# Softmax weights normalised in the output rows instead of in the probability tiles

## The chip, the cores and the metric

One core of a Trainium2 chip runs the whole program. The metric is the device time of one execution in microseconds. Times of single instructions come from one profiled execution.

## The reference

Clustered attention is followed by two MLPs. The attention has 2 batches, 8 heads, 768 positions and 64 columns a head; queries only see keys of their own cluster (the nearest of 16 centroids):

```
mask   = q_assign[:, :, :, None] == k_assign[:, :, None, :]
scores = where(mask, scale * q @ k.T, -1e9);  scores -= max(scores)
attn   = exp(scores)
attn   = attn / (sum(attn) + 1e-9)
out    = attn @ v                      # then [1536, 512]
x      = (sigmoid(x @ w_gate) * (x @ w_val)) @ w_out
x      = relu(x @ w_in)**2 @ w_out2
```

All of it is fp32 in accuracy: operands are split into a high and a low part, and products are sums of several matmuls.

## The kernel before

Heads are worked in pairs: `pairs` has 8 entries, 4 in each batch. A pair has 12 units `(i, e, n, j)`: head e of the pair, half n of the 768 query rows, and block j of 128 rows in the half. There are 96 units, and one loop over n with one iteration a unit orders the whole attention by hand (`manual_schedule`: each engine runs its instructions in the order in which the code issues them).

In iteration n the code issues, for unit n, the negated row maximum on VectorE (L934, tile nm); for the unit three iterations back (LAG = 3) two groups of three transposes on TensorE and their rounding copy on ScalarE (`evac`, L820 and L822); the scores of unit n + 1 on TensorE (L802); the exponential of unit n on ScalarE, which also sums the rows (L955); the normalisation of unit n - 1 (`normalise`: a reciprocal on VectorE, L873, and a multiplication of the 128x768 probability tile on GpSimd, L874); the low parts of the transposed tiles on VectorE (`low`, L828); and 1e-9 added to the row sums on GpSimd (L969). The transposes share a ring of three PSUM buffers (`ps_t`) with the preparation steps; the scores have two.

When the third block of a half has been transposed, three thirds of the output matmuls follow in the next three iterations (`attend`, L838 and L839). The value tile holds the high and the low part of V side by side, so an output tile has two parts of 64 rows. ScalarE copies it out of PSUM (L844), and SP moves the parts to their places (L848, L850). `finish`, some iterations later, adds the two parts on GpSimd (L858) and splits the sum into x_hi (L867) and x_lo (L869), the input of the first MLP. `SUMS` holds how many iterations later each of its steps comes.

The dictionary `late` holds work for the end of an iteration; a function that returns a `post` has that part issued at the start of the next (`drain`). The preparation of the next pair (`STEPS`; transposes of q and k, similarity to the centroids, argmax, masks) is spread over the iterations in the same way. Weight tiles of the MLPs are fetched by SP and decoded mostly on VectorE (L218 to L252); two are decoded during the first pairs of the attention, two more as it ends (`LATE_DECODES`), and the first four gated matmul groups are issued there too (`LATE_GATED`, L348 to L350). SP issues all transfers in the order of the code; a transfer that waits holds up those behind it.

Of the kernel before, what the change touches and what calls it, by code (L numbers as in the profile page):

```python
# [8 lines left out]
F32 = mybir.dt.float32  # L9
# [5 lines left out]
ALU = mybir.AluOpType  # L15
AX = mybir.AxisListType
# [44 lines left out]

EARLY_PARTS = [1, 1, 2, 2, 3, 3, 4, 9, 15, 18, 21, 22, 23, 27, 30, 31, 33, 39]
VALUES = [-3, 2, 0, 6]
SUMS = [[5, 6, 8], [6, 8, 9]]

LATE_DECODES = [1, 2]
LATE_GATED = [1, 2, 3, 3]
# [3 lines left out]
def cluster_attention_two_mlps(  # L71
# [13 lines left out]
    nc = tc.nc  # L85
    B, H, S, D = q.shape
    NCL = centroids.shape[1]
    P = 128
# [5 lines left out]
    HB = NB // 2  # L94
    NH = HB * P
# [222 lines left out]
    with tc.manual_schedule():  # L318
        ident = const.tile([P, P], F32, name="ident")
# [3 lines left out]
        ones = const.tile([P, 1], F32, name="ones")  # L323
# [129 lines left out]
        with ExitStack() as ac:  # L453
# [2 lines left out]
            nat = pc.enter_context(tc.tile_pool(name="nat", bufs=1, side="right"))  # L456
            am = pc.enter_context(tc.tile_pool(name="am", bufs=1, side="right"))
            vp = ac.enter_context(tc.tile_pool(name="vp", bufs=3))
            LAG = 3
            pp = ac.enter_context(tc.tile_pool(name="pp", bufs=LAG + 1))  # L460
            ptp = ac.enter_context(tc.tile_pool(name="ptp", bufs=2))
            sm = ac.enter_context(tc.tile_pool(name="sm", bufs=6))
            ps_t = ac.enter_context(tc.tile_pool(name="ps_t", bufs=3, space=PSUM))
            ps_o = ac.enter_context(tc.tile_pool(name="ps_o", bufs=1, space=PSUM))
            sc = ac.enter_context(ExitStack())
# [320 lines left out]


            units = [(i, e, n, j) for i in range(len(pairs)) for e in range(2) for n in range(2) for j in range(HB)]
            Pt, PThi, PTlo, xs, nms, decoding = {}, {}, {}, {}, {}, {}
            UPP, N = len(units) // len(pairs), len(units)  # L790


# [37 lines left out]
            def attend(i, e, n, third):  # L830

                if third == 0:
                    outs[i, e, n] = ps_o.tile([P, NH], F32, name="o")
                o = outs[i, e, n]
                hi, lo = PThi[i, e, n], PTlo[i, e, n]
                for c in range(third * NB // 3, (third + 1) * NB // 3):
                    vt = V[i, e][:, c].rearrange("p t d -> p (t d)")
                    nc.tensor.matmul(o, vt, hi[:, c, :], start=(c == 0), stop=False)  # L838
                    nc.tensor.matmul(o, vt, lo[:, c, :], start=False, stop=(c == NB - 1))  # L839
                if third == 2:  # L840

                    def post():
                        oc = sm.tile([P, NH], F32, name=f"oc{e}", bufs=3 - e)
                        nc.scalar.copy(oc, outs.pop((i, e, n)))  # L844
                        own, other = slice(D * e, D * e + D), slice(D - D * e, 2 * D - D * e)
                        if e == 0:
                            xs[n] = [oc, sm.tile([P, NH], F32, name="x", bufs=2)]
                        nc.sync.dma_start(out=xs[n][1][own], in_=oc[other])  # L848
                        if e == 1:
                            nc.sync.dma_start(out=xs[n][0][own], in_=oc[own])  # L850

                    return post

            def finish(i, n, t):
                b, hp = pairs[i]
                xa, xb = xs[n]
                if t == 0:
                    nc.gpsimd.tensor_tensor(out=xa, in0=xa, in1=xb, op=ALU.add)  # L858
                    return
                c0 = b * S + n * NH  # L860
                while c0 < b * S + (n + 1) * NH:
                    g = c0 // TG
                    c1 = min(b * S + (n + 1) * NH, (g + 1) * TG)
                    src = xa[:, c0 - b * S - n * NH : c1 - b * S - n * NH]
                    hi, lo = (x[:, hp, c0 - g * TG : c1 - g * TG] for x in x_in[g])
                    if t == 1:
                        nc.gpsimd.tensor_scalar(out=hi, in0=src, scalar1=1.0, scalar2=1.0, op0=ALU.mult, op1=ALU.mult)  # L867
                    else:
                        nc.gpsimd.tensor_tensor(out=lo, in0=src, in1=f32(hi), op=ALU.subtract)  # L869
                    c0 = c1  # L870

            def normalise(p, nm):
                nc.vector.reciprocal(out=nm[:, 3:4], in_=nm[:, 2:3])  # L873
                nc.gpsimd.tensor_scalar(out=p, in0=p, scalar1=nm[:, 3:4], scalar2=ones, op0=ALU.mult, op1=ALU.mult)  # L874

            load(0, "kq")
            load(1, "kq")
# [25 lines left out]
            for t, f in enumerate(prep0):  # L903
# [9 lines left out]

                keep_warm(WARM.get(t - len(prep0), 0))
            outs, late, st = {}, {}, {}
            todo = {}
            for i in range(len(pairs)):
                for m, args in zip(VALUES, ((0, 0), (0, 1), (1, 0), (1, 1))):
                    late.setdefault(max(0, i * UPP + m), []).append((values, (i, *args)))
            for i in range(1, len(pairs)):  # L920
                for m, group in (prep1 if i == 1 else prep(i)).items():
                    at = (i - 1) * UPP + m
                    todo.setdefault(at, []).append(group)
            st[0] = scores(units[0])
            for n in range(N + LAG + 4):
                u = units[n] if n < N else None
                w = units[n - LAG] if 0 <= n - LAG < N else None
                if n == N - UPP:
                    drain()
                    pc.close()  # L930
                    open_weights()
                if u is not None:
                    nms[n] = sm.tile([P, 4], F32, name="nm")
                    nc.vector.tensor_reduce(out=nms[n][:, 0:1], in_=st[n][:, :, :NH], axis=AX.XY, op=ALU.max, negate=True)  # L934
                nm = nms.pop(n - 1, None)
                if nm is not None:
                    p = Pt[units[n - 1]]
                drain()
                if nm is not None and w is None:
                    normalise(p, nm)  # L940
                if n == N:
                    sc.close()
                    for nm_, bufs in (("sg", 2), ("act", NA)):
                        pools[nm_] = ctx.enter_context(tc.tile_pool(name=nm_, bufs=bufs, side="right", reuse_waits="tile"))
                    pools["a"] = ctx.enter_context(
                        tc.tile_pool(name="ps_a", bufs=4, space=PSUM, side="right", reuse_waits="tile")
                    )
                if w is not None:
                    t0, h0 = evac(w, 0)
                    t1, h1 = evac(w, 1)  # L950
                if n + 1 < N:
                    st[n + 1] = scores(units[n + 1])
                if u is not None:
                    e = pp.tile([P, S], F32, name="p")
                    nc.scalar.activation(  # L955
                        out=e.rearrange("p (m n) -> p m n", m=2),
                        in_=st.pop(n)[:, :, :NH],
                        func=AF.Exp,
                        bias=nms[n][:, 0:1],
                        accum_out=nms[n][:, 1:2],  # L960
                    )
                    Pt[u] = e
                if w is not None:
                    if nm is not None:
                        normalise(p, nm)
                    low(w, 0, t0, h0)
                    low(w, 1, t1, h1)
                if u is not None:
                    nc.gpsimd.tensor_scalar(out=nms[n][:, 2:3], in0=nms[n][:, 1:2], scalar1=1e-9, scalar2=None, op0=ALU.add)  # L969
                if w is not None:  # L970
                    Pt.pop(w)
                    if w[3] == HB - 1:
                        end = n == N + LAG - 1
                        for t in range(3):
                            late.setdefault(n + 1 + (0 if end else t), []).append((attend, (*w[:3], t)))
                        if w[1] == 1:
                            for t in range(3):
                                at = n + SUMS[w[2]][t] if w[0] < len(pairs) - 1 else n + (3 if end else 6)
                                late.setdefault(at, []).append((finish, (w[0], w[2], t)))
                for f, args in late.pop(n, []):  # L980
                    do(f, *args)
                for m, group in enumerate(todo.pop(n, [])):
                    if m:
                        drain()
                    for f in group:
                        do(f)
                for part in decoding.pop(n, []):
                    part()
                if n - N in LATE_DECODES:
                    for t, part in enumerate(decode_next()):  # L990
                        if t < 6:
                            part()
                        else:
                            decoding.setdefault(n + 1, []).append(part)
                for t, at in enumerate(LATE_GATED):
                    if n == N + at:
                        (gated_first, gated_second)[t % 2](steps[t // 2])
# [46 lines left out]
```

## Time and profile before

| | |
|---|---|
| Median of 3 runs | 828.5 us (828.44 to 828.93) |
| Profiled execution | 829.15 us, span 827.4 us |
| TensorE matmul busy | 809.6 us (98%) |
| TensorE weight load busy | 690.7 us (83%) |
| VectorE busy | 628.4 us (76%) |
| ScalarE busy | 441.1 us (53%) |
| GpSimd busy | 214.3 us (26%), all of it in the first 280 us |

The profile comes from one execution. Matmul times overlap one another, so the rate of matmuls is read from the distance of their starts. "Idle before, releaser" gives the idle time of an engine before an instruction and whose end stopped it. PE is TensorE, PEld its weight loads, DVE VectorE, ACT ScalarE, POOL GpSimd, SPq the transfer queue of SP.

### The profile page before, as it was taken

How to read it: one execution, taken by the hardware profiler on the slowest of the kernel's cores; microseconds unless marked ns; L12 is line 12 of the kernel's file. 1: busy time of each engine (PE TensorE's matmuls, PEld its weight loads, DVE VectorE, ACT ScalarE, POOL GpSimd, SP SyncE). 2: the span in 40 equal slices, each digit the busy share in tenths (PEclk: the TensorE clock that was granted, in tenths of full speed). 3: DMA queues.
4: the chain of work that ended last, by engine and by line, in shares of the span. 5: the costliest groups of instructions: out<-in, count | busy, mean ns of one | idle time of the engine just before them, and what ended most of it. 6: DMA issues, size and time to landing. Idle time of an engine off the chain costs nothing.

```text
span 827.4 us, 11694 instructions
## 1 busy us (share of the span) xinstructions
PE 809.6 (98%) x4097; PEld 690.7 (83%) x4097; DVE 628.4 (76%) x1146; ACT 441.1 (53%) x887; POOL 214.3 (26%) x349
## 2 busy tenths in 40 slices
PE   7899999999999999999999999999999999999998
PEld 6789899999998788888888888888888888888886
DVE  6999999999898378657878757769774787788233
ACT  5778889889896223432332223246755733642530
POOL 4678899888884200000000000000000000000000
PEclk9999999999999999999999999999999999999999
DMA  8475464464321123112321212202222212221012
GB/s 198 91 158 117 98 153 104 108 139 94 81 76 37 54 70 99 51 62 69 99 77 52 77 51 77 67 10 80 74 77 76 77 51 76 77 77 52 0 51 101
DMA packets 63274, 67.01 MB, mean 81 GB/s; under 512 B 28624, under 2 KB 54224, under 8 KB 63216
## 3 DMA queue, kind: packets, MB, share of 16 engines
q1 hardware_dynamic: 63216, 66.27, 29.4%
q8 instruction: 32, 0.52, 0.3%
q14 instruction: 26, 0.21, 0.1%
HBM read 45.12 MB, written 3.15 MB: 58 GB/s over the span
## 4 chain that ended last, share of the span: by engine, by line
PE 80%; DVE 13%; POOL 2%; ACT 2%; issue 2%; DMA 1%; SPq 0%; POOLq 0%; DVEq 0%; ACTq 0%
PE bank_b L426 18%; PE bank_a L349 13%; PE bank_a L348 13%; PE bank_a L350 13%; PE bank_a L426 9%; DVE pt_lo L828 4%; PE t L820 4%; DVE nm L934 4%; PE s L802 4%; PE o L838 2%; PE o L839 2%; DMA oc<-oc 1%; PE t L617 1%; POOL p L874 1%; PE t L562 1%
## 5 line engine op out<-in xcount | busy, mean ns | idle before, releaser
L349 PE MATMUL bank_a<-x_lo,w 128*128 128x512 f32 x480 | 189.5, 395 | 0.9 <-POOL x_lo L869 0.9
L348 PE MATMUL bank_a<-x_hi,w 128*128 128x512 f32 x480 | 188.3, 392 | 0.1
L350 PE MATMUL bank_a<-x_hi,w 128*128 128x512 f32 x480 | 187.7, 391 | 0.0
L392 DVE TENSOR_TENSOR slo<-act,shi 128x512 fp32r<-128x512 f32 x84 | 57.8, 688 | 69.2 <-ACT shi L391 64.9
L348 PEld LDWEIGHTS bank_a<-x_hi,w 128*128 128x128 f32 x480 | 90.1, 188 | 21.3 <-POOL x_hi L867 0.5
L349 PEld LDWEIGHTS bank_a<-x_lo,w 128*128 128x128 f32 x480 | 90.1, 188 | 20.9 <-POOL x_lo L869 1.2
L350 PEld LDWEIGHTS bank_a<-x_hi,w 128*128 128x128 f32 x480 | 90.2, 188 | 20.1
L828 DVE TENSOR_TENSOR pt_lo<-t,pt_hi 128x384 fp32r<-128x384 f32 x192 | 96.7, 544 | 7.8 <-ACT pt_hi L822 7.7
L874 POOL TENSOR_SCALAR p<-p,nm,ones 128x768 f32<-128x768 f32 x96 | 94.9, 989 | 16.8 <-DVE nm L873 15.0
L955 ACT ACTIVATE p<-s,nm 128x768 f32<-128x768 f32 x96 | 88.0, 916 | 18.0 <-DVE nm L873 10.4
L802 PE MATMUL s<-st_k,st_q 128*128 128x384 f32 (+1 forms) x384 | 91.8, 362 | 1.9 <-ACT p L955 1.9
L934 DVE TENSOR_REDUCE nm<-s 128x1 f32<-128x768 f32 x96 | 90.8, 946 | 0.0
L822 ACT CAST pt_hi<-t 128x384 fp32r<-128x384 f32 x192 | 83.3, 488 | 6.9 <-PE t L820 6.5
L820 PE MATMUL t<-ident,p 128*128 128x128 f32 x576 | 82.2, 277 | 3.7 <-DVE pt_lo L828 2.3
L391 ACT CAST shi<-act 128x512 fp32r<-128x512 f32 x84 | 51.6, 615 | 58.2 <-PE bank_b L426 34.6
L426 PE MATMUL bank_b<-wo,shi 128*128 128x512 f32 x256 | 79.0, 390 | 0.0
L230 ACT CAST w<-wtop 128x512 fp32r<-128x512 f32 x38 | 23.7, 622 | 102.6 <-DVE wtop L248 102.6
L820 PEld LDWEIGHTS t<-ident,p 128*128 128x128 f32 x576 | 66.7, 141 | 11.2 <-issue 3.7
L374 DVE TENSOR_TENSOR act<-bank_a,sg 128x512 f32<-128x512 f32 x36 | 24.9, 691 | 55.5 <-PE bank_a L350 51.2
L802 PEld LDWEIGHTS s<-st_k,st_q 128*128 128x128 f32 (+1 forms) x384 | 63.2, 191 | 4.5 <-ACT p L955 4.2
L838 PE MATMUL o<-pt_hi,vt 128*128 128x384 f32 x192 | 65.2, 339 | 0.4 <-ACT oc L844 0.4
L839 PE MATMUL o<-pt_lo,vt 128*128 128x384 f32 x192 | 64.7, 337 | 0.0
(137 smaller groups left out, 1385.6 us busy)
## 6 DMA issues: line engine op xcount, KB each, us to landing
wraw<-in_moe_w_out_dram SPq DMA_DIRECT2D x28, 512.0 KB, 3.3
wraw<-in_moe_w_in_dram SPq DMA_DIRECT2D x16, 512.0 KB, 3.9
wraw<-in_moe_w_gate_dram SPq DMA_DIRECT2D x11, 512.0 KB, 3.6
wraw<-in_moe_w_val_dram SPq DMA_DIRECT2D x11, 512.0 KB, 3.6
nat_v<-in_v_dram SPq DMA_DIRECT2D x8, 384.0 KB, 3.4
st_k<-st_k SPq DMA_DIRECT2D x16, 192.0 KB, 4.8
x<-oc SPq DMA_DIRECT2D x32, 96.0 KB, 2.1
out_dram<-part SPq DMA_DIRECT2D x12, 256.0 KB, 2.1
```

The lines of the kernel that those rows point to most:

```text
L348: nc.tensor.matmul(bk, w[:, 0, ks], mov_hi[:, kk], start=(kk == 0), stop=False)
L349: nc.tensor.matmul(bk, w[:, 0, ks], mov_lo[:, kk], start=False, stop=False)
L350: nc.tensor.matmul(bk, w[:, 1, ks], mov_hi[:, kk], start=False, stop=(kk == KD - 1))
L426: nc.tensor.matmul(bk, st, mv, start=(first and n == 0), stop=(last and n == 2))
L802: nc.tensor.matmul(st[:, m, :NH], Q[i, e][: DEPTH[e][a], a, c * P : (c + 1) * P], K[i, e][: DEPTH[e][a], a, m * NH : (m + 1) * NH], start= ...
L820: nc.tensor.transpose(tp[:, m, :], Pt[u][:, c * P : (c + 1) * P], ident)
L822: nc.scalar.copy(hi, tp)
L828: nc.vector.tensor_tensor(out=lo, in0=tp, in1=f32(hi), op=ALU.subtract)
L838: nc.tensor.matmul(o, vt, hi[:, c, :], start=(c == 0), stop=False)
L874: nc.gpsimd.tensor_scalar(out=p, in0=p, scalar1=nm[:, 3:4], scalar2=ones, op0=ALU.mult, op1=ALU.mult)
L934: nc.vector.tensor_reduce(out=nms[n][:, 0:1], in_=st[n][:, :, :NH], axis=AX.XY, op=ALU.max, negate=True)
L955: nc.scalar.activation(out=e.rearrange("p (m n) -> p m n", m=2), in_=st.pop(n)[:, :, :NH], func=AF.Exp, bias=nms[n][:, 0:1], accum_out=nms ...
```

## The change

The probability tiles stay unnormalised. The row sums of a half, three blocks of two heads, are collected in one tile of 128x6 (`sums`). `reciprocals` does the rest in three steps, spread over iterations by `RECIPROCALS`: step 0 adds 1e-9 and takes the reciprocal on VectorE; step 1 transposes the 128x6 tile on TensorE into a buffer of `ps_t`, and its post copies it on ScalarE and writes it to DRAM as two rows of 384; step 2 reads each row back, broadcast to 64 partitions. `finish` gets a fourth step, a multiplication of the output by this tile on GpSimd. The normalisation and its reciprocals go, LAG becomes 2, and `SUMS` is set anew.

```diff
-SUMS = [[5, 6, 8], [6, 8, 9]]
+SUMS = [[6, 7, 8, 9], [6, 7, 9, 10]]
+RECIPROCALS = [(1, 4, 5), (1, 2, 3)]
...
-            LAG = 3
+            LAG = 2
...
+            rows = ac.enter_context(tc.tile_pool(name="rows", bufs=2, space=bass.MemoryType.DRAM))
...
+                if t == 1:
+                    nc.gpsimd.tensor_tensor(out=xa, in0=xa, in1=recips.pop((i, n)), op=ALU.mult)
+                    return
...
-            def normalise(p, nm):
-                nc.vector.reciprocal(out=nm[:, 3:4], in_=nm[:, 2:3])
-                nc.gpsimd.tensor_scalar(out=p, in0=p, scalar1=nm[:, 3:4], scalar2=ones, op0=ALU.mult, op1=ALU.mult)
+            def reciprocals(i, n, t):
+                if t == 0:
+                    ss = sums[i, n]
+                    nc.vector.tensor_scalar(out=ss, in0=ss, scalar1=1e-9, scalar2=None, op0=ALU.add)
+                    nc.vector.reciprocal(out=ss, in_=ss)
+                elif t == 1:
+                    tr = ps_t.tile([2 * HB, P], F32, name="t")
+                    nc.tensor.transpose(tr, sums.pop((i, n)), ident)
+                    def post():
+                        recips[i, n] = sm.tile([P, NH], F32, name="rc", bufs=2)
+                        rr = recips[i, n][: 2 * HB, :P]
+                        nc.scalar.copy(rr, tr)
+                        by_row[i, n] = rows.tile([2, NH], F32, name="r")
+                        nc.sync.dma_start(out=by_row[i, n].rearrange("e (j p) -> (e j) p", p=P), in_=rr)
+                    return post
+                else:
+                    rc = recips[i, n]
+                    src = by_row.pop((i, n))
+                    for h in range(2):
+                        nc.sync.dma_start(out=rc[D * h : D * h + D], in_=src[h : h + 1].to_broadcast([D, NH]))
...
-                        accum_out=nms[n][:, 1:2],
+                        accum_out=sums[u[0], u[2]][:, HB * u[1] + u[3] :][:, :1],
...
-                    nc.gpsimd.tensor_scalar(out=nms[n][:, 2:3], in0=nms[n][:, 1:2], scalar1=1e-9, scalar2=None, op0=ALU.add)
+                if u is not None and u[1] == 1 and u[3] == HB - 1:
+                    for t, at in enumerate((0, 1, 2) if n == N - 1 else RECIPROCALS[u[2]]):
+                        late.setdefault(n + at, []).append((reciprocals, (u[0], u[2], t)))
```

## Rows read from the trace of the kernel before

**Rows 1.** The page's first part: busy us, share of the span, instructions.
```profile
PE 809.6 (98%) x4097; PEld 690.7 (83%) x4097; DVE 628.4 (76%) x1146; ACT 441.1 (53%) x887; POOL 214.3 (26%) x349
```

**Rows 2.** Busy time by stretch: stretch, length; PE, PEld, DVE, ACT, POOL; clock, DMA, GB/s.
```profile
19.30:45.00 25.70, 21.27 (x123) 17.60 (x122) 24.80 (x48) 18.52 (x44) 16.01 (x24) 0.93 0.49 121
150.90:180.20 29.30, 29.00 (x201) 27.91 (x200) 27.33 (x59) 25.88 (x62) 25.05 (x40) 1.00 0.53 121
```

**Rows 3.** Timeline of VectorE (start, length): maxima of units 12, 24, 48 and 60.
```profile
52.55 0.95 DVE L934 TENSOR_REDUCE nm<-s 128x1 f32<-128x768 f32 x1
84.42 0.94 DVE L934 TENSOR_REDUCE nm<-s 128x1 f32<-128x768 f32 x1
143.54 0.95 DVE L934 TENSOR_REDUCE nm<-s 128x1 f32<-128x768 f32 x1
172.91 0.95 DVE L934 TENSOR_REDUCE nm<-s 128x1 f32<-128x768 f32 x1
```

**Rows 4.** Chain that ended last, in pair 4: start, us on the chain, what.
```profile
151.76 0.87 DVE nm L934
155.96 0.67 PE t L820 x6
156.63 0.71 PE s L802 x4
```

**Rows 5.** Instruction groups, first 330 us: busy us, mean ns | idle before, releasers.
```profile
L874 POOL TENSOR_SCALAR p<-p,nm,ones 128x768 f32<-128x768 f32 x96 | 94.9, 989 | 16.8 <-DVE nm L873 15.0 <-PE o L839 0.7 <-PE s L802 0.6
L873 DVE RECIPROCAL nm<-nm 128x1 f32<-128x1 f32 x96 | 14.7, 153 | 6.2 <-POOL nm L969 5.9
```

**Rows 6.** Decode lines L248 and L241, 15 to 300 us: ns min/median/max, first, last.
```profile
L248 DVE SCALAR_TENSOR_TENSOR wtop<-wmag,wbody x5: 682/693/696, 259.5 to 298.0; 128x512 f32<-128x512 f32 x5
L248 DVE SCALAR_TENSOR_TENSOR spare<-spare x2: 852/1104/1357, 26.1 to 83.6; 128x512 f32<-128x512 f32 x2
...
L241 DVE TENSOR_SCALAR wbody<-wraw x5: 416/421/1102, 258.3 to 296.8; 128x512 int32<-128x512 int32 x5
```

**Rows 7.** Timeline around the maxima of units 18 and 19.
```profile
66.76 1.01 POOL L858 TENSOR_TENSOR oc<-oc,x 128x384 f32<-128x384 f32 x1 [0.98 <-DMA oc<-oc]
...
67.28 0.94 DVE L934 TENSOR_REDUCE nm<-s 128x1 f32<-128x768 f32 x1
...
69.53 0.16 DVE L873 RECIPROCAL nm<-nm 128x1 f32<-128x1 f32 x1 [0.84 <-POOL nm L969]
...
69.61 1.00 DVE L828 TENSOR_TENSOR pt_lo<-t,pt_hi 128x384 fp32r<-128x384 f32 x2
...
71.26 0.94 DVE L934 TENSOR_REDUCE nm<-s 128x1 f32<-128x768 f32 x1
```

**Rows 8.** Timeline at the end of pair 7: maxima of units 92 to 94.
```profile
245.81 0.95 DVE L934 TENSOR_REDUCE nm<-s 128x1 f32<-128x768 f32 x1
...
248.16 0.95 DVE L934 TENSOR_REDUCE nm<-s 128x1 f32<-128x768 f32 x1
...
249.65 0.16 DVE L873 RECIPROCAL nm<-nm 128x1 f32<-128x1 f32 x1 [0.55 <-POOL nm L969]
...
250.67 0.95 DVE L934 TENSOR_REDUCE nm<-s 128x1 f32<-128x768 f32 x1
```

**Rows 9.** Timeline from the attention's end into the first MLP.
```profile
262.94 0.49 ACT L844 COPY oc<-o 128x384 f32<-128x384 f32 x1
...
267.42 0.37 SPq L192 DMA_DIRECT2D wraw<-in_moe_w_val_dram  x1
...
267.85 0.51 SPq L848 DMA_DIRECT2D x<-oc  x1
...
272.93 1.01 POOL L858 TENSOR_TENSOR oc<-oc,x 128x384 f32<-128x384 f32 x1 [15.38 <-DMA oc<-oc]
...
275.92 0.50 PE L349 MATMUL bank_a<-x_lo,w 128*128 128x512 f32 x1 [0.88 <-POOL x_lo L869]
```

**Rows 10.** The page's part on transfers: count, KB each, median us to landing.
```profile
x<-oc SPq DMA_DIRECT2D x32, 96.0 KB, 2.1
```

More of the change, by code (lines that the diff above doesn't have):

```diff
@@ L788, in cluster_attention_two_mlps @@
             units = [(i, e, n, j) for i in range(len(pairs)) for e in range(2) for n in range(2) for j in range(HB)]
-            Pt, PThi, PTlo, xs, nms, decoding = {}, {}, {}, {}, {}, {}
+            Pt, PThi, PTlo, xs, decoding = {}, {}, {}, {}, {}
             UPP, N = len(units) // len(pairs), len(units)
@@ L846, in post @@
                         if e == 0:
-                            xs[n] = [oc, sm.tile([P, NH], F32, name="x", bufs=2)]
-                        nc.sync.dma_start(out=xs[n][1][own], in_=oc[other])
+                            xs[i, n] = [oc, sm.tile([P, NH], F32, name="x", bufs=2)]
+                        nc.sync.dma_start(out=xs[i, n][1][own], in_=oc[other])
                         if e == 1:
-                            nc.sync.dma_start(out=xs[n][0][own], in_=oc[own])
+                            nc.sync.dma_start(out=xs[i, n][0][own], in_=oc[own])
                     return post
@@ L855, in finish @@
                 b, hp = pairs[i]
-                xa, xb = xs[n]
+                xa, xb = xs[i, n]
                 if t == 0:
                     nc.gpsimd.tensor_tensor(out=xa, in0=xa, in1=xb, op=ALU.add)
+                    return
+                if t == 1:
+                    nc.gpsimd.tensor_tensor(out=xa, in0=xa, in1=recips.pop((i, n)), op=ALU.mult)
                     return
@@ L865, in finish @@
                     hi, lo = (x[:, hp, c0 - g * TG : c1 - g * TG] for x in x_in[g])
-                    if t == 1:
+                    if t == 2:
                         nc.gpsimd.tensor_scalar(out=hi, in0=src, scalar1=1.0, scalar2=1.0, op0=ALU.mult, op1=ALU.mult)
@@ L915, in cluster_attention_two_mlps @@
             outs, late, st = {}, {}, {}
+            sums, by_row, recips = {}, {}, {}
             todo = {}
@@ L932, in cluster_attention_two_mlps @@
                 if u is not None:
[L933 to L937, printed above, removed]
+                    nm = sm.tile([P, 1], F32, name="nm")
+                    nc.vector.tensor_reduce(out=nm, in_=st[n][:, :, :NH], axis=AX.XY, op=ALU.max, negate=True)
                 drain()
-                if nm is not None and w is None:
-                    normalise(p, nm)
                 if n == N:
@@ L953, in cluster_attention_two_mlps @@
                 if u is not None:
+                    if u[1] == 0 and u[3] == 0:
+                        sums[u[0], u[2]] = sm.tile([P, 2 * HB], F32, name="sums", bufs=4)
                     e = pp.tile([P, S], F32, name="p")
@@ L958, in cluster_attention_two_mlps @@
                         func=AF.Exp,
-                        bias=nms[n][:, 0:1],
-                        accum_out=nms[n][:, 1:2],
+                        bias=nm,
+                        accum_out=sums[u[0], u[2]][:, HB * u[1] + u[3] :][:, :1],
                     )
@@ L963, in cluster_attention_two_mlps @@
                 if w is not None:
-                    if nm is not None:
-                        normalise(p, nm)
                     low(w, 0, t0, h0)
                     low(w, 1, t1, h1)
-                if u is not None:
-                    nc.gpsimd.tensor_scalar(out=nms[n][:, 2:3], in0=nms[n][:, 1:2], scalar1=1e-9, scalar2=None, op0=ALU.add)
+                if u is not None and u[1] == 1 and u[3] == HB - 1:
+                    for t, at in enumerate((0, 1, 2) if n == N - 1 else RECIPROCALS[u[2]]):
+                        late.setdefault(n + at, []).append((reciprocals, (u[0], u[2], t)))
                 if w is not None:
@@ L976, in cluster_attention_two_mlps @@
                         if w[1] == 1:
-                            for t in range(3):
+                            for t in range(4):
                                 at = n + SUMS[w[2]][t] if w[0] < len(pairs) - 1 else n + (3 if end else 6)
```

## Prediction

> **What bounds the kernel now.** I read the page's totals first, then the same totals by stretch, then the chain of waits inside the attention part, and last the timeline at the places where the chain leaves TensorE. The totals have TensorE busy for 98% of the span [rows 1], which would leave nothing to win. The stretches say otherwise: in a middle pair weight loads fill 27.91 of 29.30 us, in the first 25.70 us only 17.60, and there it is VectorE that is full, 24.80 us [rows 2]. So the limits differ by stage. A pair is 12 units, each opened by one maximum on VectorE. Pair 1 lasts 84.42 - 52.55 = 31.9 us, pair 4 only 172.91 - 143.54 = 29.4 us, 2.45 us a unit [rows 3]. In pair 4 the chain runs over VectorE until 151.76 (units 0 to 3, where the argmax steps of the next pair lie) and over TensorE behind it, where six transposes take 0.67 us and four score matmuls 0.71 us [rows 4]. The two MLPs, the 550 us behind the attention, are full on TensorE and the diff doesn't touch them. Only some 250 us can change.
>
> Matmul busy time is no good measure of how near TensorE is to its limit, says the Trainium skill (Trainium Kernel Development and Optimization, "Performance Expectations"), and weight-load time is one. The rows agree: 98% of the span against 17.60 of 25.70 us in the head. By busy time alone every added transpose would cost its full time and nothing could be won; by weight loads the head has room.
>
> **What goes.** 96 normalisations on GpSimd, 94.9 us, 989 ns each, and 96 reciprocals on VectorE, 14.7 us [rows 5]; the addition of 1e-9 goes too. A reciprocal is listed at 0.16 us, but the instruction behind it starts 0.08 us after it (69.53 to 69.61) [rows 7]: it holds VectorE for 0.08 us, so all 96 together are worth 7.7 us of VectorE at most, and less where TensorE is the limit. What matters more is that GpSimd drops out of the way from a probability tile to its transposes; LAG falls from 3 to 2 with it.
>
> *Head, units 0 to 11*, where VectorE is the limit: 12 reciprocals x 0.08 = 1.0 us gained. The decode step L248 takes 1357 ns there and 682 to 696 later with GpSimd quiet [rows 6]: 0.7 us gained if the normalisation was what it collided with, 0 if another GpSimd operation was; I take 0.7, since normalisations are the largest part of GpSimd's work, 94.9 of 214.3 us [rows 1, 5]. Against that, LAG 2 brings one unit's two subtractions in before unit 12 that came behind it, 1.00 us [rows 7]. Sum -0.7.
>
> That collision is a rule of the Trainium skill (SBUF — State Buffer, "Who interferes with whom"): a VectorE instruction with two SBUF inputs contends with a GpSimd one that reads SBUF, and the later one waits. L248 has two such inputs and the rows agree, 1357 against 682 ns. The rule also speaks against the change: its new multiplications on GpSimd lie beside weight decoding in the tail, where a one-input L241 already once took 1102 instead of 416 ns [rows 6]. By the rule the sum would be 0.7 us worse if one such decode were late for TensorE.
>
> *Pair 1.* From unit 18 to 19 it takes 71.26 - 67.28 = 3.98 us instead of 2.45. The reason is in the rows: GpSimd's sum that joins the two value parts of an output waited 0.98 us for a transfer, the operations queued behind it came late, and the reciprocal of this unit waited 0.84 us for GpSimd, with both subtractions behind it [rows 7]. This goes twice over: no probability tile waits for GpSimd, and this sum moves from one unit behind its transfer to two. 1.5 us. Of its 12 reciprocals (1.0 us) I count half, since TensorE takes over in part of the pair. Sum -2.0; that leaves pair 1 at 29.9, still over the 29.4 of pair 4, because it carries decode steps.
>
> *Pairs 2 to 5.* Per pair, four reciprocals leave the VectorE stretch (0.3 us), and one addition and one reciprocal on 128x6 come into it, two dependent ones of 0.15 each [rows 5], 0.3 us. The two new transposes on TensorE cost 0.67 / 6 = 0.11 us each [rows 4]; they are issued in units 0 and 1 of the next pair, where VectorE is late and TensorE waits anyway. Cost nothing; if that cover is gone, 0.2 us a pair, 1.8 us for all 16. Sum 0, between -0.3 and +0.5 a pair.
>
> *Pairs 6 and 7* have no or little preparation, and a unit is worth 0.67 + 0.71 of TensorE [rows 4] and again 0.71 for its third of the output matmuls (as many columns as the scores): 2.1 us. But two units at the end of pair 7 take 2.35 and 2.51 us, and the reciprocal there waits 0.55 us for GpSimd [rows 8], which then has normalisations, values and finishing steps back to back. 0.65 us gained there, and as much in pair 6, whose units 80 to 83 look alike. Sum -1.3.
>
> *Tail.* Behind the last maximum there is one transposition group and one third of an output less, 0.67 + 0.71 = 1.4 us of TensorE, which went into the head where TensorE is idle. And TensorE waits 0.88 us for the low half of the attention output (x_lo) [rows 9]: the output copy that the transfer moves was started at 262.94, but the transfer sits on SP until 267.85, behind a weight fetch at 267.42. With LAG 2 the transfer is issued one step earlier, ahead of that second fetch, so this wait goes: -0.9. The new multiplication on GpSimd puts 1.0 us (the size of the sum, 1.01 [rows 9]) into the same chain for each half, but the chain starts up to 4.4 us earlier (262.94 + 0.49 to 267.85). If that gain is lost to the queue, the tail is 1.0 us worse instead of 0.9 better. Sum -2.3.
>
> *What else is added.* ACT copies 6x128 sixteen times: between 0 and the 0.49 us of a 128x384 copy [rows 9]; I take 0.2, near a third of it for a third of the columns, in units where ACT isn't last, so nothing on the path; with no cover 16 x 0.2 = 3 us in all. Transfers: 16 writes and 32 broadcast reads through DRAM. SP issues in order, so the reads stand on it until the write has landed: by the nearest row 2.1 us [rows 10], and as much again for the read. Queued behind them are the copies of the next output rows, and stacks and mask rows of the next pair; GpSimd waits for the first two or more units later (4.9 us), TensorE for the others eight units later. Hidden; a miss delays only GpSimd, which nothing urgent follows now. At the last unit the added VectorE pair waits for the exponential that has just been issued, with one subtraction behind it: 0 to 1 us, inside a stretch in which TensorE has the gated matmuls next.
>
> **The sum.** -0.7 - 2.0 + 0 - 1.3 - 2.3 = -6.3 us. The profiled execution took 829.15, so 822.85; it lies 0.65 above the median of the runs, which makes 822.2.
>
> **Rivals.**
> (a) *TensorE is the limit all along.* For it: 98% in [rows 1]; against it: the head's weight loads. Then the stalls of VectorE and GpSimd are made up later anyway, only the x_lo wait goes, and 16 transposes come: -0.9 + 1.8 = +0.9, 829.4 by the median. No change by the 0.2% (1.7 us) that a measurement of this kernel can tell.
> (b) *The transposes' PSUM ring becomes the wait: slower.* Three buffers hold them, a unit takes two, and the new small transpose takes the third in 16 units, so the next unit's first group can't start until this unit's subtraction on VectorE is done. It decides if VectorE is left idle for the way around: it costs 0.5 us each (half of a subtraction pair, 1.00 [rows 7]) x 16 = 8 us, against the -6.3: +1.7, 830.2 by the median; from 0.4 us each it eats the gain. Against it: most units with a preparation step already use all three, and still the TensorE part of pair 4 goes at 2.4 us a unit.
> (c) *VectorE gets all of it back.* If the middle pairs also run faster by their reciprocals (12 x 0.08 = 1.0 us a pair, four pairs), 818.2. Against it: there TensorE is full [rows 2].
> (d) *The factors arrive late, so the change does not take GpSimd off the path:* SP's waits of 2 x 2.1 us hold up what is queued behind them. In the pairs the stacks have eight units of room; in the tail it would cost the 0.9 us again and 4.2 us once: 822.2 + 5.1 = 827.3.
>
> **Chances.** Forecast 0.58, (a) 0.13, (b) 0.11, (c) 0.12, (d) 0.06. Faster by over 0.2%: 0.58 + 0.12 + half of (d) and a little of (a) = 0.75; slower: (b) and a little = 0.12; the same 0.13. The forecast alone spans 819.5 to 825.5 (the bounds of the terms above). To leave out no more than 2 in 10, the range goes from 818.0 to 829.0.
>
> **What would show it.** The unit 18 to 19 interval near 2.5 us and pair 1 under 30.2; pair 4 still 29.1 to 29.8, with the chain as before (if it grows by over 0.5, (b)); units 92 to 94 at 2.1; the maximum of unit 94 near 246.7 instead of 250.67 (-0.7, -2.0, -1.3); no wait of TensorE for x_lo; L248 in the head near 0.7. I am wrong if the middle pairs move by over 0.5 us each, or if the reads of the factors stand in front of a stack transfer that a score matmul waits for.

## The result, and the profile after

The changed kernel takes 833.16 us (median of 4 runs, 831.97 to 834.57), the kernel before 828.71: a ratio of 1.0052 (95% interval 1.0038 to 1.0066). It is slower by half a per cent, where 6.3 us less were forecast; it lies above the range of 818.0 to 829.0.

The profiled execution has a span of 832.0 us against 827.4. The totals say little, as they did before [rows 1]: GpSimd lost half its work, and no other engine gained.

```profile
PE 811.4 (98%) x4113; PEld 691.6 (83%) x4113; DVE 630.8 (76%) x1082; ACT 443.9 (53%) x903; POOL 111.5 (13%) x173
```

VectorE has 64 instructions less and is 2.4 us busier: something on it got longer. The maxima that open the pairs show where the time went. From the timeline of VectorE (start, length; units 12, 24, 48, 60, 72 and 95), to be read against [rows 3]:

```profile
51.60 0.95 DVE L961 TENSOR_REDUCE nm<-s 128x1 f32<-128x768 f32 x1
84.28 0.95 DVE L961 TENSOR_REDUCE nm<-s 128x1 f32<-128x768 f32 x1
145.17 0.95 DVE L961 TENSOR_REDUCE nm<-s 128x1 f32<-128x768 f32 x1
175.19 0.95 DVE L961 TENSOR_REDUCE nm<-s 128x1 f32<-128x768 f32 x1
209.13 0.95 DVE L961 TENSOR_REDUCE nm<-s 128x1 f32<-128x768 f32 x1
258.70 0.95 DVE L961 TENSOR_REDUCE nm<-s 128x1 f32<-128x768 f32 x1
```

From such starts comes a ledger of the span, one profiled execution a column, in us (the two right columns are the experiments e3 and e5 below). The tail runs from the maximum of unit 95 to the end of the span.

| stretch | before | after | e3 | e5 |
|---|---|---|---|---|
| start to unit 0 | 19.2 | 19.8 | 19.7 | 19.9 |
| pair 0 (head) | 33.3 | 31.8 | 31.8 | 31.8 |
| pair 1 | 31.9 | 32.7 | 31.9 | 29.8 |
| pairs 2 to 4 | 88.5 | 90.9 | 88.7 | 87.8 |
| pair 5 | 29.3 | 33.9 | 29.2 | 29.2 |
| pair 6 | 27.5 | 26.7 | 26.5 | 26.5 |
| unit 84 to 95 | 23.3 | 22.9 | 22.9 | 22.9 |
| tail | 574.4 | 573.3 | 573.3 | 573.2 |

The head, pair 6, the end of pair 7 and the tail gained. Pair 5 alone lost 4.6 us, pairs 2 to 4 lost 2.4, pair 1 lost 0.8 instead of gaining 2.0. Two things in the timeline account for most of it.

**The new addition stands behind GpSimd.** The timeline in unit 57 (VectorE and GpSimd): x_hi and x_lo are split on GpSimd; the addition of 1e-9 on a 128x6 tile starts at 169.54 and ends at 170.95, with the second x_lo (169.77 + 1.14 = 170.91).

```profile
169.14 0.66 POOL L873 TENSOR_SCALAR x_hi<-oc 128x128 fp32r<-128x128 f32 x2
...
169.54 1.41 DVE L882 TENSOR_SCALAR sums<-sums 128x6 f32<-128x6 f32 x1
...
169.77 1.14 POOL L875 TENSOR_TENSOR x_lo<-oc,x_hi 128x128 fp32r<-128x128 f32 x2
...
170.98 0.19 DVE L883 RECIPROCAL sums<-sums 128x6 f32<-128x6 f32 x1
171.09 0.92 DVE L961 TENSOR_REDUCE nm<-s 128x1 f32<-128x768 f32 x1
```

All 16 additions, shortest, median and longest in ns:

```profile
L882 DVE TENSOR_SCALAR sums<-sums x16: 160/164/1675, 45.7 to 261.2; 128x6 f32<-128x6 f32 x16
```

Sixteen of the shortest would be busy for 2.6 us. They are busy for 7.8: six of them, in the first halves of their pairs, took 0.28 to 1.68.

**SP stands on its own write.** SP's queue in pair 5 (start of the issue, length). The write of the factors is followed by their two reads, which SP can't issue before the write has landed; the transfer of the low part of q, st_q<-lo_q, comes 12.8 us after pair 5 opens (188.00 - 175.19). Before, it came 5.4 us after that (178.35 - 172.91 [rows 3]). Last line: before.

```profile
178.16 1.42 SPq L893 DMA_DIRECT2D r<-rc  x1
181.84 1.10 SPq L900 DMA_DIRECT2D rc<-r  x2
...
184.32 0.43 SPq L893 DMA_DIRECT2D r<-rc  x1
186.16 1.10 SPq L900 DMA_DIRECT2D rc<-r  x2
187.31 0.59 SPq L602 DMA_DIRECT2D st_k<-st_k  x1
188.00 0.54 SPq L602 DMA_DIRECT2D st_q<-lo_q  x1
```

```profile
178.35 0.46 SPq L599 DMA_DIRECT2D st_q<-lo_q  x1
```

In pairs 6 and 7 lo_q has a single buffer, so the next pair's low part can't be written until that transfer has read the old one. VectorE waits 2.90 us, TensorE 2.38 behind it, and then TensorE's granted clock is 0.50 (the 1.2 GHz level) for 3.4 us. The profile names no releaser for VectorE's wait ("issue"); that it is this buffer follows from the order here, and e11 tests it. Timeline, and behind it busy time by stretch (columns as in [rows 2]):

```profile
191.65 0.56 DVE L571 SCALAR_TENSOR_TENSOR lo_q<-t,st_q 128x384 fp32r<-128x384 f32 x1 [2.90 <-issue]
...
192.27 0.55 PE L565 MATMUL t<-ident,nat_k 128*128 128x128 f32 x3 [2.38 <-DVE lo_q L571]
```

```profile
19.30:45.00 25.70, 22.11 (x141) 19.22 (x140) 25.11 (x44) 21.05 (x49) 5.08 (x8) 1.00 0.53 130
...
193.40:196.80 3.40, 3.40 (x13) 3.40 (x12) 2.86 (x5) 1.76 (x4) 2.01 (x2) 0.50 0.46 129
```

The 2.4 us wait and the slow stretch are nearly all of the 4.6 us of pair 5: unit 65, with the wait, took 5.25 us and unit 67, with the slow stretch, 3.96, where the run e2 below has 2.48 and 2.39. (The head's first stretch, 0.93 before [rows 2], now runs at 1.00. That is not where the head's gain comes from: the two units in which the clock was 0.50 before took 3.29 and 2.12 us, and 3.30 and 2.12 at full clock in e7 below.)

### The profile page after: what moved, and what is told of

Same layout as the page of the kernel before. It is cut to its first block, busy times and chain, and to the rows that moved or that the text cites. A ratio compares the mean times of both kernels' runs of the same rounds, so it can differ in the third digit from the quotient of the medians.

```text
span 832.0 us, 11408 instructions
## 1 busy us (share of the span) xinstructions
PE 811.4 (98%) x4113; PEld 691.6 (83%) x4113; DVE 630.8 (76%) x1082; ACT 443.9 (53%) x903; POOL 111.5 (13%) x173
## 4 chain that ended last, share of the span: by engine, by line
PE 67%; DMA 0%; DVE 0%; SPq 0%; ACT 0%; issue 0%
PE bank_b L427 18%; PE bank_a L350 13%; PE bank_a L349 13%; PE bank_a L351 13%; PE bank_a L427 9%; DMA rc<-r 0%; SPq L900 0%; PE o L841 0%; DMA r<-rc 0%; PE o L842 0%; DVE wo L237 0%; DVE slo L393 0%; DVE part L433 0%; ACT shi L392 0%; DVE wtop L234 0%; DVE wbody L222 0%
## 5 line engine op out<-in xcount | busy, mean ns | idle before, releaser
L350 PEld LDWEIGHTS bank_a<-x_lo,w 128*128 128x128 f32 x480 | 90.1, 188 | 19.8
L427 PE MATMUL bank_b<-shi,wo 128*128 128x512 f32 x192 | 60.3, 390 | 0.2 <-DVE wo L237 0.2
```

The lines of the kernel that those rows point to most:

```text
L350: nc.tensor.matmul(bk, w[:, 0, ks], mov_lo[:, kk], start=False, stop=False)
L427: nc.tensor.matmul(bk, st, mv, start=(first and n == 0), stop=(last and n == 2))
```

## The experiments

Theory A: the loss is VectorE's addition, blocked behind GpSimd. Theory B: it is SP's wait, through the transfers behind it. Times are medians, with the ratio to runs of the kernel before on the same chip. The median of the kernel before differs by up to 0.7 us between the sets of runs (828.71 to 829.44), so runs of different sets are better compared by their ratios; the changed kernel's is 1.0052.

**e1: no addition.** The row sums are at least 1, so 1e-9 is lost in their rounding.

```diff
-                    nc.vector.tensor_scalar(out=ss, in0=ss, scalar1=1e-9, scalar2=None, op0=ALU.add)
```

> Leaves out the addition of 1e-9 to the row sums on VectorE (the reciprocal alone stays). Theory A (the addition is blocked behind GpSimd operations: 16 of them hold VectorE 7.8 us, 2.6 us without the collisions) expects most of those 5.2 us back plus the additions themselves: 833.2 - 4.5 = 828.7, and intervals of units 9 to 10 at about 2.5 us instead of 3.8. Theory B (the loss is SP's wait for the write, which holds up the stack transfers behind it) expects 0.6 us at most: 832.6, with the 5.25 us interval of unit 65 still there.

830.36 us, 1.0009 (1.0000 to 1.0017): 2.8 us less than the changed kernel by the medians, 0.43% or 3.6 us by the ratios. A is right in part, and less than it expected; the intervals of units 33, 45 and 57 fell from 3.3, 3.8 and 3.8 us to 2.4, but pair 5 still took 33.3 us.

**e2: later reads.**

```diff
-RECIPROCALS = [(1, 4, 5), (1, 2, 3)]
+RECIPROCALS = [(1, 4, 6), (1, 2, 4)]
```

> Issues the broadcast reads one iteration later for both halves (RECIPROCALS (1,4,6) and (1,2,4)), when their write has landed, so that SP does not stand on them. Theory B expects the low-q buffer's wait in pair 5 (2.9 us) and the clock drop behind it (1.5 us) to go: 833.2 - 4.5 = 828.7, pair 5 back to 29.5 to 30.5 us. Theory A alone expects no change, 833, with pair 5 still long by some other cause.

829.24 us, 1.0003 (0.9995 to 1.0012): 3.9 us less by the medians, 0.49% or 4.1 us by the ratios. The transfer of lo_q comes 9.0 us after pair 5 opens (184.04 - 175.00), and VectorE no longer waits for it. Pair 5 is 204.40 - 175.00 = 29.4 us:

```profile
175.00 0.95 DVE L961 TENSOR_REDUCE nm<-s 128x1 f32<-128x768 f32 x1
...
204.40 0.95 DVE L961 TENSOR_REDUCE nm<-s 128x1 f32<-128x768 f32 x1
```

**e3: both edits.**

> Both edits: no addition, and the later reads. If A and B are both true and add, 833.2 - 9 = 824; if they are the same loss seen twice, 828 to 829; if neither, 832 to 833.

825.63 us, 0.9957 (0.9945 to 0.9970). 7.5 us less than the changed kernel, where the two alone gave 2.8 and 3.9; by the ratios 0.95%, where the two alone gave 0.43 and 0.49. They add up: two losses, not one seen twice. Where the addition was stretched to 1675 ns, the reciprocal alone now runs beside x_hi:

```profile
76.37 0.66 POOL L873 TENSOR_SCALAR x_hi<-oc 128x128 fp32r<-128x128 f32 x2
...
76.77 0.18 DVE L882 RECIPROCAL sums<-sums 128x6 f32<-128x6 f32 x1
```

**e4: no chain of reciprocals at all.**

```diff
-                    nc.gpsimd.tensor_tensor(out=xa, in0=xa, in1=recips.pop((i, n)), op=ALU.mult)
+                    nc.gpsimd.tensor_tensor(out=xa, in0=xa, in1=xb, op=ALU.mult)
...
-                    for t, at in enumerate((0, 1, 2) if n == N - 1 else RECIPROCALS[u[2]]):
-                        late.setdefault(n + at, []).append((reciprocals, (u[0], u[2], t)))
```

> Leaves out the whole chain of the reciprocals (addition, reciprocal, transpose, copy, write and reads) and so the normalisation itself: finish multiplies by another tile of the same size in its place. It is the floor of this change. A and B together explain the loss if it is at most 1.5 us faster than the run with both edits (about 823). If something else (LAG 2, the free-running GpSimd) costs the time, it stays above 827.

825.45 us, 0.9955 (0.9941 to 0.9968), the same as e3 within the intervals. Once the addition and the wait are gone, the rest of the chain (16 reciprocals, transposes and copies, 48 transfers) costs nothing that these intervals can tell, as forecast.

**e5: decode parts moved.** e3 still has pair 1 at 31.9 us. There and in pair 3 the one-hot step on VectorE (oh, which marks each position's cluster), with two SBUF inputs, was stretched from 0.56 to 1.5 us by a decode operation of GpSimd; before, GpSimd was held up by normalisations and came to it 3 us later.

```diff
-EARLY_PARTS = [1, 1, 2, 2, 3, 3, 4, 9, 15, 18, 21, 22, 23, 27, 30, 31, 33, 39]
+EARLY_PARTS = [1, 1, 2, 2, 3, 3, 4, 9, 16, 18, 20, 22, 23, 27, 30, 31, 33, 40]
```

> The run with both edits (825.6), and beside it three decode parts of the first two weight tiles moved by one unit (15 to 16, 21 to 20, 39 to 40 in EARLY_PARTS). Theory C (GpSimd, no longer paced by the normalisations, runs ahead in bursts that block VectorE operations which need the shared port: one-hot at units 14 and 38, 1.46 to 1.53 us instead of 0.58, and decode line L219 at unit 21, 1.57 instead of 0.4) expects -0.9 -0.9 -1.1 = -2.9: 822.7, with the intervals of units 14, 38 and 21 near 2.9, 2.9 and 2.7. The rival (TensorE or ScalarE is next at once) expects 825 to 825.6 with those intervals hardly shorter.

824.01 us, 0.9930 (0.9918 to 0.9942). Pair 1 is 29.8 us, pair 3 29.2 instead of 30.1; the ledger gives 3.0 us for the 2.9 of theory C. The medians give 1.6 and the ratios 0.27%, 2.2 us; the intervals of e3 and e5 lie close but do not overlap, so the step is there, smaller in the times than in the two profiles. The kernel before was not run with the moved parts. Its unit 21 took 3.45 us too, where e5 has 2.36, so some of this may be had without the change. The one-hot step in e3 and then in e5 (ns):

```profile
L681 DVE TENSOR_TENSOR oh<-eq,m x8: 557/558/1535, 16.2 to 208.9; 128x384 bf16<-128x384 f32 x8
```

```profile
L681 DVE TENSOR_TENSOR oh<-eq,m x8: 557/558/559, 16.4 to 206.1; 128x384 bf16<-128x384 f32 x8
```

**e6: the addition kept, two units later.**

```diff
-RECIPROCALS = [(1, 4, 5), (1, 2, 3)]
+RECIPROCALS = [(3, 4, 6), (1, 2, 4)]
```

> The run with the later reads (829.2), with the addition kept, but the addition and reciprocal of the first half issued two units later (unit 11 instead of 9 of the pair), away from the burst of x_hi and x_lo on GpSimd. Theory A (the addition is blocked by GpSimd) expects about the collisions back, -2.5 to -3: 826.5. Its rival (the addition and its dependent reciprocal cost VectorE their time wherever they stand, and leaving them out gains that) expects 829, no change.

827.74 us, 0.9979 (0.9970 to 0.9987); e2, which differs only in the place of the addition, had 1.0003. So the collision costs about 0.24%, 2 us, less than expected. The remaining 0.22%, 1.8 us, between this and e3 go with the additions themselves; there the two intervals just touch. None is stretched any more:

```profile
L882 DVE TENSOR_SCALAR sums<-sums x16: 155/160/172, 51.6 to 254.9; 128x6 f32<-128x6 f32 x16
```

**e7: the kernel before with the shorter lag alone.**

```diff
-            LAG = 3
+            LAG = 2
```

> The kernel before with LAG = 2 alone; the normalisation in the probability tiles stays. If the shorter lag is what gains in the head and the tail (as the forecast has it: 1.4 us of TensorE moved into the head, 0.9 us of the x_lo wait), it is 1 to 2.3 us faster: 827. If the lag of 3 was needed to cover the way over GpSimd, transposes wait for normalised tiles, and it is slower: 831 to 835. Then the change pays by taking GpSimd out, not by the lag alone.

845.95 us, 1.0199 (1.0185 to 1.0212), slower by far more than either side had it. (The edit also takes the probability tiles from four buffers to three, bufs=LAG + 1, as in the changed kernel; the two are not told apart.) Waits from 20 to 270 us (engine and line, for whom: us in total, times, longest): TensorE's transposes wait for the normalised tile in most units.

```profile
PEld t L820 <- POOL p L874: 34.8, 60, 1.8
...
PE t L820 <- POOL p L874: 16.6, 30, 1.5
```

**e8: the output copy of the tail earlier.** Where TensorE waited 0.88 us for x_lo [rows 9], it now waits for the single output bank (the one PSUM buffer of the output tiles, which ScalarE copies out). The timeline of the changed kernel:

```profile
267.80 0.44 PE L841 MATMUL o<-pt_hi,vt 128*128 128x384 f32 x1 [1.06 <-ACT oc L847]
```

```diff
                 for f, args in late.pop(n, []):
                     do(f, *args)
+                if n > N:
+                    drain()
```

> The run with both edits (825.6), with the output copy of the last but one half issued right behind its matmuls instead of behind the sigmoid. If the wait of TensorE for the single output bank (1.06 us, where before it waited 0.88 us for x_lo) is what ate the gain of the tail, 825.6 - 1.1 = 824.5. If the x_lo or the next weight comes late in its place, no change: 825.6.

829.11 us, 0.9990 (0.9980 to 1.0000), 0.33% or 2.7 us worse than e3. The wait went, and another came: ScalarE now makes the output copy ahead of a step of the weight decode, and TensorE waits 2.58 us for the weight; from 270.8 to 274.1 its granted clock is then 0.50. The tail is 576.3 us in place of 573.3.

```profile
269.49 0.82 DVE L237 TENSOR_TENSOR w<-wtop,wbody 128x512 fp32r<-128x512 f32 x1
...
270.37 0.50 PE L351 MATMUL bank_a<-x_hi,w 128*128 128x512 f32 x1 [2.58 <-DVE w L237]
```

**e9: e4 with the lag of 3.**

```diff
-            LAG = 2
+            LAG = 3
```

> The run that leaves out the chain and the normalisation (825.45), with LAG = 3 in place of 2. The forecast gave the shorter lag 1.4 us (transposes and a third of the output matmuls moved from tail to head) less 1.0 in the head, and the x_lo wait of 0.9: if so 826.5 to 827.7. If the lag by itself is worth nothing, and it was only GpSimd's leaving that gained, 825.5.

824.86 us, 0.9941 (0.9929 to 0.9954): no slower than e4. The maxima of units 12 and 95, first e4, then e9:

```profile
51.44 0.95 DVE L961 TENSOR_REDUCE nm<-s 128x1 f32<-128x768 f32 x1
...
250.46 0.95 DVE L961 TENSOR_REDUCE nm<-s 128x1 f32<-128x768 f32 x1
```

```profile
50.80 0.95 DVE L961 TENSOR_REDUCE nm<-s 128x1 f32<-128x768 f32 x1
...
248.11 0.95 DVE L961 TENSOR_REDUCE nm<-s 128x1 f32<-128x768 f32 x1
```

With LAG 3 the last maximum comes 2.35 us earlier, and the tail (to spans of 823.2 and 822.9) is 2.0 us longer. The tail's gain by the lag is real and is paid back in full ahead of it.

**e10: e5 with the last decodes earlier,** and the early copy in iteration N + 1 alone.

```diff
-LATE_DECODES = [1, 2]
+LATE_DECODES = [0, 1]
...
+                if n == N + 1:
+                    drain()
```

> The run with the moved decode parts (824.0), and in the tail both last decodes one iteration earlier (LATE_DECODES 0 and 1) and the output copy of the first half issued right behind its matmuls in iteration N + 1 alone. The early copy by itself cost time because the weight came 2.6 us late; if the decode is what the tail then waits for, this gives 824.0 - 1.1 = 823. If three us of decode on VectorE ahead of the last subtractions are late instead, 824.5 to 826.

822.98 us, 0.9920 (0.9907 to 0.9933). The interval overlaps with that of e5, so the step isn't shown; the trace has TensorE waiting 0.9 us for x_lo again, in place of the output bank.

**e11: the changed kernel with two buffers for lo_q.**

```diff
-                    return pools["hl"].tile([P, S], F32R, name="lo_q")
+                    return pools["hl"].tile([P, S], F32R, name="lo_q", bufs=2)
```

> The changed kernel as it is (833.2), with two buffers instead of one for the low part of q (lo_q) in pairs 6 and 7; the reads stay where they hold up SP. If SP's wait hurts only because the one lo_q buffer isn't free (2.9 us) and the clock falls behind it (1.5 us), 833.2 - 4.5 = 828.7, as with the later reads. If the late stacks hurt elsewhere too, it stays above 831.

829.70 us, 1.0000 (0.9992 to 1.0008), as with the later reads, and pair 5 is 204.77 - 175.15 = 29.6 us. SP still stands on its writes; with room for lo_q that costs nothing that shows. Theory B holds through this one buffer: 0.52% by the ratios, as much as e2 within the intervals.

## Why the prediction was wrong, step by step

- **The step that failed most: "TensorE for the others eight units later. Hidden; a miss delays only GpSimd".** SP's wait was named, 2.1 us a landing, and rival (d) was built on it with 0.06. But for the transfers behind it only the side of the readers was counted (when a score matmul needs the stack), not that of the source: lo_q must be read out before the next pair writes it, three units after the issue. With two waits of SP ahead of it that transfer came 7.4 us later in its pair than before (12.8 us in, not 5.4), and the write waited. It cost 4.6 us by the ledger, 4.1 by e2, 4.3 by e11. The forecast's own sign of being wrong was a score matmul that waits for its stack; what waited was the step that overwrites the source.
- **"Two dependent ones of 0.15 each, 0.3 us" for the addition and the reciprocal, "sum 0" for pairs 2 to 5.** The addition took up to 1.68 us, and pair 4 grew to 30.0, over the 29.8 that the forecast allowed; that was its sign for rival (b), but without the addition (e3) pair 4 is back at 29.3. The forecast quoted the rule of the Trainium skill (SBUF — State Buffer, "Who interferes with whom") for L248 and for the tail, and did not put it to the instruction that the change itself adds. The same section says that a tensor_scalar can take the shared port in its fast mode and then collides with GpSimd. The rows agree: 160 ns alone, 1675 beside x_lo, while the reciprocal, 0.19 us, wasn't stretched once; in e3 it takes 0.18 in the same place, beside x_hi. Taking the addition out gained 3.6 us (e1 by the ratios, and e2 to e3); moving it, 2 (e6).
- **"GpSimd drops out of the way": it also stops being paced.** With half its work it runs ahead of the loop and its bursts land on other VectorE steps. That is why pair 1 gained nothing in e3 although most of its stall had gone (unit 18 to 19: 2.59 us after and 2.89 in e3, instead of 3.98 [rows 7]). Only with three decode parts moved is pair 1 at 29.8. That this meets the 29.9 of the forecast is partly luck: against before, unit 18 gave 1.0 of the 1.5 (2.95 us in e5), and units 20 and 21 another 0.6.
- **"Sum -2.3" for the tail and "-0.7" for the head.** The tail gained 1.1: the x_lo wait went and one for the output bank of 1.06 took its place. The shorter lag gave the tail its 2.0 (e9) but cost 2.35 ahead of it, not 1.0: 0.9 in the head, about as forecast, and the rest in the pairs, where the forecast had nothing. It isn't needed; e7 shows that it only became possible. The head gained 1.5, after a start that came 0.6 later.
- **Right:** the stall of unit 18; L248 in the head, 0.69 us after (it is L249 there); pairs 6 and 7, -1.4 in e5 for -1.3; the transposes, copies and transfers hidden (e4); rival (b), the ring of PSUM buffers, didn't come; nor did (a): with the two side costs gone the kernel is faster by 0.43% (e3), and with the decode parts moved by 0.70% (e5). (c) didn't come either: without the addition pairs 2 and 4 are 0.3 and 0.1 us shorter, not 1.0 each.

A gain near the forecast one can be had: e5 has a span of 821.2, 6.2 us under the one before (5.8 by the ratio), where the sum was 6.3. That the two agree so well is in part luck. e5 has neither the addition nor the early reads, it owes 2 to 3 us to the three moved decode parts, and by stage the tail gained 1.2 less than forecast and pairs 2 to 5, from which nothing was forecast, 0.8. Without the moved parts the gain is 3.5 us (e3). What the sum left out was what the added instructions wait for and whom they hold up. Not settled: why the addition costs another 1.8 us where it doesn't collide (e6 to e3); sixteen at 0.16 to 0.2 us would be 2.6 to 3.2 if none were hidden, and that none is hidden wasn't shown.

## What to carry to other kernels

Put each rule on contention to the instructions that a change adds before those that it removes, and ask of each transfer behind a new wait not only who reads its target but who wants to overwrite its source. A read-back through DRAM belongs at least one loop step behind its write on an in-order queue. When an engine is relieved, its remaining work moves in time: look at what it will then run beside.

## What the runs showed of the hardware that was not expected

- A 128x6 addition on VectorE took from 155 to 1675 ns; moved away from x_hi and x_lo on GpSimd (e6), none took over 172.
- The way through DRAM took 181.84 - 178.16 = 3.7 us from the issue of the write to that of the read, where the forecast had 2.1, and the next one 1.8 us (184.32 to 186.16). The write's issue took 1.42 us of the first and 0.43 of the second. Four stack transfers were issued just ahead of the first; that they made it longer is not shown.
- A wait of TensorE of 2.38 us was followed by 3.4 us at a granted clock of 0.50; from unit 67 to 68 that made 3.96 us of 2.40. In e8 the same came behind a wait of 2.58 us.
